# Pooled attention with a multiplicative FFN on one core: the FFN's products in 64-row tiles between the scores, attention in bursts of one head, a ring of exponentials twice as long

## The chip, the core and the metric

One Trainium2 chip, one of its cores, one launch. The metric is device time in microseconds (us): the median of the runs of the kernel. The engines are named as the profile names them: PE is TensorE (matmuls), PEld its weight loads, DVE is VectorE, ACT is ScalarE, POOL is GpSimd, SP is SyncE, which here only issues DMAs.

## The reference

Inputs are float32. q, k and v are [8 batches, 8 heads, 1152 positions, 64]. The FFN works on 4608 tokens (8 batches of 576), d_model 512, d_ff 1024.

```python
q_pool = q.reshape(B, H, S // 2, 2, D).mean(axis=3)          # 576 queries a head
scores = (1 / sqrt(D)) * q_pool @ k.T                        # 576 x 1152 a head
attn = softmax(scores, axis=-1)
x = (attn @ v).transpose(0, 2, 1, 3).reshape(B * 576, H * D) # 4608 x 512
h = ((x @ w1) * (x @ w2)) @ w3                               # 4608 x 1024
out = h @ w_out                                              # 4608 x 512
```

The kernel never forms h: it computes T = w3 @ w_out once (1024 x 512), and out = ((x @ w1) * (x @ w2)) @ T.

## The kernel before

**Pairs, steps and chunks.** Two heads of a batch make a pair P (32 pairs). The 1152 keys of a head are cut into 9 blocks of 128, and a pair has 9 steps (NJ), each of 576 queries (SQ) against one key block, for both heads. The steps of all pairs follow each other as one line of 32 x 9 x 576 columns, which is cut into 324 chunks of 512 columns (CH). A pair is 10.125 chunks long.

**Scores and exponentials.** `scores(c)` (line 229) makes one chunk: for each of the one or two steps that it touches, one matmul per head. A head has 64 features, so each is a matmul on 64 of the 128 rows of PE: head 0 on rows 0 to 63, head 1 on rows 64 to 127, into two PSUM banks of a tile `psc`, of which there are two (4 banks). `expo(c)` (line 235) is one ACT instruction over 128 x 1024 elements, from `psc` to a ring `er` in SBUF, which holds 9 chunks (RING 4608). PE can write a chunk's scores when ACT has read the chunk two before it.

**Attention times V.** `attend(J, i)` (line 248) takes 128 exponentials columns as weights and 65 columns of V (the 65th holds a constant, so that it sums the exponentials), on all 128 rows, for both heads. Its accumulator `po` has two banks, one per head. A pair has 9 x 5 x 2 = 90 of these matmuls, and there are 2880. After the last step of a pair `normalize(P)` takes the reciprocal (line 258) and multiplies (line 260) on DVE, and two DMA transposes (lines 265, 268) put the result into `xT`, the FFN's input.

**Keys and queries.** For the first nine pairs `prep_pe` (lines 203, 155) transposes queries and keys on PE through two PSUM banks, and DVE copies them out (lines 209 to 211). Later pairs go through DMA transposes (lines 131, 133). POOL issues the loads from HBM; `wosb` (w_out) and `w3h` (w3) are loaded early, `w1sb` and `w2sb` after them.

**The FFN.** It works in units of 512 tokens, nine in all (`gen_ffn`). A unit has 8 pairs of gate blocks: `pa` (line 347) is four matmuls on 128 rows with 512 columns, copied to SBUF by DVE (line 356); `pb` (line 360) is four, multiplied by that copy (line 365) into `gT`. Then come four row blocks `pp` (line 373) of eight matmuls each, scaled into SBUF (line 382) and stored by DMA (line 387). A unit thus has 96 matmuls. A unit can run when its tokens' pairs are done; seven units run beside the attention, and the last two and what is left of the seventh after it. All PSUM tiles of the FFN, of T (`gen_T`, line 313) and of the transposes of w3 (line 302) share two banks (tag `ff`).

**The order.** It is written out by hand, in the order of the code, for each engine. The loop goes over 162 iterations of two chunks: scores of both chunks, then the `attend` matmuls that are ready, then FFN matmuls as `fill` takes them from a list of generators, one matmul at a time, until a planned time `due` is reached, which grows by PACE0 or PACE1 (2.2, 2.19 us) an iteration. So a block of four FFN matmuls may be split over two iterations.

**PSUM** has 8 banks: 4 for `psc`, 2 for `ff`, 2 for `po`.

Of the kernel before, what the change touches and what calls it, by code (L numbers as in the profile page):

```python
# [10 lines left out]
ALU = mybir.AluOpType  # L11
# [7 lines left out]
RING = 4608  # L19
# [4 lines left out]
def kernel(  # L24
# [21 lines left out]
    T_MM, T_TR, T_SC, T_AV, T_PREP = 0.216, 0.06, 0.63, 0.061, 1.0  # L46
    PACE0, PACE1 = 2.2, 2.19
# [13 lines left out]
    w3T = const.tile([128, NF, NF, 128], FP16)  # L61
# [5 lines left out]
    seen = const.tile([1, 2], FP16)  # L67

# [6 lines left out]
    kst, vst, qst, kT, qT, qps = {}, {}, {}, {}, {}, {}  # L75

# [81 lines left out]
    def prep_first():  # L158
# [6 lines left out]
        ta = psum.tile([128, 1024], FP16, tag="ff", bufs=2, name="ta")  # L165
        tb = psum.tile([128, 1024], FP16, tag="ff", bufs=2, name="tb")
# [30 lines left out]
    def prep_pe(P):  # L197
        pp, o = P // 2, 64 * (P % 2)
        new_kq(P)
        t2 = psum.tile([128, 1024], FP16, tag="ff", bufs=2, name="t2")  # L200
        t1 = psum.tile([128, 1024], FP16, tag="ff", bufs=2, name="t1")
        for c in range(NJ):
            nc.tensor.transpose(t2[:, 128 + 64 * c:192 + 64 * c],  # L203
                                qps[pp][o:o + 64, c].rearrange("p u d -> p (u d)"),
                                ident[o:o + 64, o:o + 64])
        keys(P, t2, range(8, 9))
        keys(P, t1, range(0, 8))
        del kcs[P]
        nc.vector.tensor_copy(out=qT[P].rearrange("p c f -> p (c f)"), in_=t2[:, 128:704])
        nc.vector.tensor_copy(out=kT[P][:, 0:8].rearrange("p j f -> p (j f)"), in_=t1)  # L210
        nc.vector.tensor_copy(out=kT[P][:, 8], in_=t2[:, 0:128])
# [26 lines left out]
    po = {}  # L238

    def attend(J, i):  # L240

        P, j = divmod(J, NJ)
        if j == 0 and i == 0:
            po[P] = psum.tile([128, 2, 512], FP32, tag="po", bufs=1, name="po")
        f = 128 * i if i < 4 else SQ - 128
        r = (J * SQ) % RING + f
        for u in range(2):
            nc.tensor.matmul(  # L248
                po[P][:, u, VW * i:VW * i + D + 1],
                er[:, u, r:r + 128],  # L250
                vts[P % 4][:, u, j, 0:D + 1],
                start=(j == 0 and i == 0), stop=(j == NJ - 1 and i == 4),
                skip_group_check=True)

    def normalize(P):
        acc = po.pop(P)[:, :, 0:5 * VW].rearrange("p u (i w) -> p u i w", w=VW)
        rz = ab.tile([128, 2, 5, 1], FP32, tag="rz", bufs=2, name="rz")
        nc.vector.reciprocal(out=rz, in_=acc[:, :, :, D:D + 1])
        xn = ab.tile([128, 5, 2, D], FP16, tag="xn", bufs=3, name="xn")
        nc.vector.tensor_tensor(  # L260
            out=xn.rearrange("p i u d -> p u i d"), in0=acc[:, :, :, 0:D],
            in1=rz.to_broadcast([128, 2, 5, D]), op=ALU.mult)
# [7 lines left out]
            in_=xn[64:128, 4].rearrange("p u d -> p (u d)"))  # L270

# [22 lines left out]
    def bank(pre, wide):  # L294
        if not wide:
            return psum.tile([128, 512], FP32, tag="ff", bufs=2, name=pre)
        return psum.tile([128, 2, 512], FP32, tag="psc", bufs=2, name=pre)[:, 0, :]

    def w3_transpose(c):
        t = psum.tile([128, 1024], FP16, tag="ff", bufs=2, name="w3t")  # L300
        for a in range(NF):
            nc.tensor.transpose(t[:, 128 * a:128 * a + 128],  # L302
                                w3h[c // 4][:, c % 4, 128 * a:128 * a + 128], ident)
        nc.vector.tensor_copy(out=w3T[:, c].rearrange("p a f -> p (a f)"), in_=t)

    def gen_w3(c):
        w3_transpose(c)
        yield 8 * T_TR, 0

    def gen_T(c):  # L310
        pt = bank("pT", False)
        for a in range(NF):
            nc.tensor.matmul(pt, w3T[:, c, a, :], wosb[:, a, :],  # L313
                             start=(a == 0), stop=(a == NF - 1))
            if a < NF - 1:
                yield T_MM, NF - 1 - a
        nc.vector.tensor_copy(out=T16[:, c, :], in_=pt)
        yield T_MM, 0

    def last_rows(pp, gT, r0):  # L320
        osb = ffp.tile([128, dm], FP32, tag="osb", bufs=3, name="osb")
        for h in range(2):
            hs = slice(256 * h, 256 * h + 256)
            if h == 1:
                pp = bank("pp", False)
# [15 lines left out]
    def gen_ffn(t, tail):  # L341
        t0 = 512 * t
        gT = ffp.tile([128, NF, 512], FP16, tag="g", name="gT")
        for ft in range(NF):
            pa = bank("pa", tail and ft % 2)
            for mc in range(NC):
# [3 lines left out]
                if mc < NC - 1:  # L350
                    yield T_MM, NC - 1 - mc
            asb = ffp.tile([128, 512], FP32, tag="asb", name="asb")
            if tail:
                nc.scalar.copy(out=asb, in_=pa)  # L354
            else:
                nc.vector.tensor_copy(out=asb, in_=pa)  # L356
            yield T_MM, 0
            pb = bank("pb", tail and ft % 2)
            for mc in range(NC):
# [3 lines left out]
                if mc < NC - 1:  # L363
                    yield T_MM, NC - 1 - mc
            nc.vector.tensor_mul(out=gT[:, ft, :], in0=pb, in1=asb)  # L365
            yield T_MM, 0
        for i in range(4):
            pp = bank("pp", tail and i % 2)
            if tail and t == n_units - 1 and i == 3:
                last_rows(pp, gT, t0 + 384)  # L370
                return
            for ft in range(NF):
                nc.tensor.matmul(pp, gT[:, ft, 128 * i:128 * i + 128], T16[:, ft, :],  # L373
                                 start=(ft == 0), stop=(ft == NF - 1))
                if ft < NF - 1:
                    yield T_MM, NF - 1 - ft
            osb = ffp.tile([128, dm], FP32, tag="osb", bufs=3, name="osb")
            if tail:
                nc.scalar.activation(out=osb, in_=pp, func=AF.Copy, bias=0.0,
                                     scale=1.0 / (SCL * SCL))  # L380
            else:
                nc.vector.tensor_scalar_mul(out=osb, in0=pp, scalar1=1.0 / (SCL * SCL))  # L382

            for s in range(2):
                b, f = divmod(t0 + 128 * i + 64 * s, SQ)
                rows = out[b * SQ:(b + 1) * SQ, :].rearrange("(p c) m -> c p m", c=NJ)
                nc.sync.dma_start(out=rows[f // 64], in_=osb[64 * s:64 * s + 64, :])
            yield T_MM, 0
# [3 lines left out]
    NIT = NCHUNK // 2  # L392
# [19 lines left out]
    filler = []  # L412
    next_unit = 0
    busy = due = 0.0
    left = 0
    blocks = [(J, i) for J in range(NP * NJ) for i in range(5)]
    nb = 0

    def fill(until, settle=False):

        nonlocal busy, left
        while filler and (left if settle else busy < until):
            try:
                cost, left = next(filler[0])
                busy += cost
            except StopIteration:
                filler.pop(0)

    early = [(5, gen_w3, 0), (5, gen_w3, 1), (9, gen_T, 0), (9, gen_T, 1),
             (10, gen_w3, 2), (10, gen_w3, 3), (10, gen_T, 2), (11, gen_T, 3),  # L430
             (14, gen_w3, 4), (15, gen_w3, 5), (15, gen_T, 4), (15, gen_w3, 6),
             (15, gen_T, 5), (15, gen_w3, 7), (15, gen_T, 6), (15, gen_T, 7)]

    def pv(ready):
        for J, i in ready:
            attend(J, i)

    STAGE = {1: 0.39, 2: 1.35}
    PREP = {1: 0.55, 2: 1.5}
    closed = False  # L440
    for it in range(NIT):
        at = it * 2 * CH / PAIR
        while early and it >= early[0][0]:
            _, gen, c = early.pop(0)
            filler.append(gen(c))
        while next_unit < n_units:
            last_b = (512 * (next_unit + 1) - 1) // SQ
            if (last_b + 1) * 4 * PAIR + 3 * 2 * CH > it * 2 * CH:
                break
            filler.append(gen_ffn(next_unit, False))  # L450
            next_unit += 1
        ready = [b for b in blocks[nb:nb + 40]
                 if b[0] * SQ + min(128 * b[1] + 128, SQ) <= 2 * it * CH]
        last = [n for n, (J, i) in enumerate(ready) if J % NJ == NJ - 1 and i == 4]
        if last:
            ready = ready[:last[0] + 1]
        nb += len(ready)
        half = 0 if filler else len(ready) // 2
        scores(2 * it)
        expo(2 * it)  # L460
        if it == 0:
# [4 lines left out]
        pv(ready[:half])  # L466
        scores(2 * it + 1)
        expo(2 * it + 1)
        busy += T_SC
        due = (due if filler else busy - T_SC) + (PACE0 if it < 20 else PACE1)  # L470
        if it >= NIT - 6:
            due -= 0.25
# [20 lines left out]
        if todo or (last and left <= 2):  # L493
            fill(0, settle=True)
        elif closed:
            fill(min(due - T_AV * len(ready), busy + 3 * T_MM))
        closed = bool(last)
        pv(ready[half:])
        busy += T_AV * len(ready)
        if last:  # L500
            normalize(ready[-1][0] // NJ)
        if todo:
            prep_pe(prepped)
            busy += T_PREP
            prepped += 1
        else:
            fill(due)
    fill(0, settle=True)
    for J, i in blocks[nb:]:
        attend(J, i)  # L510
    normalize(NP - 1)
    for g in filler:
        for _ in g:
            pass
    while next_unit < n_units:
        for _ in gen_ffn(next_unit, True):
            pass
# [31 lines left out]
```

## Time and profile before

| what | value |
|---|---|
| median of 3 runs (lowest, highest) | 435.61 us (435.55, 436.33) |
| span of the profiled execution, first to last instruction | 433.2 us |
| granted TensorE clock over the span | 0.999 |
| PE busy | 418.4 us, 97% |
| ACT busy | 329.2 us, 76% |
| DVE busy | 208.6 us, 48% |
| POOL busy | 84.4 us, 19% |
| exponentials (ACT, line 235) | 324, from 8.3 us to the last start at 372.1 us |
| FFN matmuls, all lines | 856 of 512 columns and 16 of 256 |
| DVE reading one FFN bank of 512 columns | 690 ns |

The execution that was profiled has no time of its own apart from its span; the median lies 2.4 us above the span, and the working below takes these 2.4 us as fixed.

The page gives an engine's busy time as the union of its instructions. A matmul's duration there (379 ns for 512 columns) is from its first column in to its last result out, and the next one starts before that; what one costs in a row of them is the distance from start to start, which is read from the timeline. In the timeline equal instructions are merged: start, time from the first start to the last end, and the count.

### The profile page before, as it was taken

The page shows a single profiled execution, that of the slowest core. Times are in us where ns is not written, and L with a number is a line of the kernel's source. Part 1 is how long each engine was busy: PE and PEld are TensorE (multiplying, and loading weights), DVE is VectorE, ACT ScalarE, POOL GpSimd, SP SyncE. Part 2 cuts the span into 40 slices and gives each one's busy share as a digit, 9 for nine tenths or more (in the row PEclk, how much of TensorE's full clock was granted, in tenths as well). Part 3 has the DMA queues.
Part 4 walks back from the last instruction along what each step waited for, and adds up shares of the span by engine and source line. Part 5 has one row for each costly group of instructions (what it writes and reads, how often), then busy time and mean ns, then how long its engine had stood idle before and what let it go on. Part 6 is the DMA issues. An engine that isn't in the chain of part 4 may idle for free.

```text
span 433.2 us, 12222 instructions
## 1 busy us (share of the span) xinstructions
PE 418.4 (97%) x5194; PEld 226.5 (52%) x5194; DVE 208.6 (48%) x365; ACT 329.2 (76%) x351; POOL 84.4 (19%) x154
## 2 busy tenths in 40 slices
PE   4899999999999999999999999999999999999996
PEld 2556666555555555555555555555545555444443
DVE  2445555575455544545356545554465433544131
ACT  4998888878888888888888888888888888403332
POOL 8313333002222040122222222222222000000000
PEclk9999999999999999999999999999999999999999
DMA  8999999908999999999899899999979972030404
GB/s 122 205 196 199 190 190 204 176 15 115 144 176 134 143 139 201 152 143 124 164 176 135 133 159 182 142 144 136 196 129 138 147 120 39 17 80 17 98 1 97
DMA packets 94197, 58.67 MB, mean 135 GB/s; under 512 B 64832, under 2 KB 84544, under 8 KB 94144
## 3 DMA queue, kind: packets, MB, share of 16 engines
q0 software_dynamic: 26528, 33.56, 51.1%
q1 hardware_dynamic: 67456, 24.22, 34.7%
q8 instruction: 40, 0.66, 0.7%
q10 hardware_dynamic: 160, 0.13, 0.1%
q14 instruction: 13, 0.11, 0.1%
HBM read 67.11 MB, written 9.44 MB: 177 GB/s over the span
## 4 chain that ended last, share of the span: by engine, by line
PE 90%; ACT 4%; issue 2%; DMA 1%; DVE 1%; POOL 0%; SPq 0%; ACTq 0%; POOLq 0%
PE po L248 21%; PE psc L229 21%; PE pa L347 14%; PE pp L373 14%; PE pb L360 14%; ACT er L235 4%; PE pT L313 3%; PE t L155 1%; DMA kst<-in_k_dram 1%; PE w3t L302 1%; PE t L203 1%; DMA out_dram<-osb 1%; DVE xn L260 0%; PE tb L155 0%; POOL qst L82 0%
## 5 line engine op out<-in xcount | busy, mean ns | idle before, releaser
L235 ACT ACTIVATE er<-psc 128x1024 f16<-128x1024 f32 x324 | 313.0, 1021 | 52.8 <-PE psc L229 50.1
L248 PEld LDWEIGHTS <-er 128*128 128x128 f16 x2880 | 100.4, 97 | 36.8 <-issue 26.8
L248 PE MATMUL po<-vt,er 128*128 128x65 f16 x2880 | 116.4, 194 | 0.1
L229 PE MATMUL psc<-qT,kT 64*128 64x512 f16 (+7 forms) x1152 | 109.7, 288 | 4.6 <-ACT er L235 3.2
L229 PEld LDWEIGHTS <-kT 64*128 64x128 f16 x1152 | 43.9, 94 | 77.0 <-issue 65.5
L365 DVE TENSOR_TENSOR gT<-pb,asb 128x512 f16<-128x512 f32 x72 | 49.7, 690 | 69.4 <-PE pb L360 69.4
L360 PE MATMUL pb<-xT,w2sb 128*128 128x512 f16 x288 | 80.7, 379 | 0.1
L347 PE MATMUL pa<-xT,w1sb 128*128 128x512 f16 x288 | 79.4, 379 | 0.0
L373 PE MATMUL pp<-T,gT 128*128 128x512 f16 x280 | 69.3, 379 | 0.0
L356 DVE COPY asb<-pa 128x512 f32<-128x512 f32 x56 | 38.6, 690 | 42.7 <-PE pa L347 42.7
L382 DVE TENSOR_SCALAR osb<-pp 128x512 f32<-128x512 f32 x28 | 19.3, 690 | 47.2 <-PE pp L373 47.2
L347 PEld LDWEIGHTS <-w1sb 128*128 128x128 f16 x288 | 25.4, 97 | 25.6 <-issue 3.2
L138 POOL COPY seen<-kT 1x1 f16<-1x1 f16 x21 | 5.3, 250 | 170.0 <-DMA kT<-kc 170.0
L360 PEld LDWEIGHTS <-w2sb 128*128 128x128 f16 x288 | 25.0, 97 | 24.3 <-issue 3.9
L373 PEld LDWEIGHTS <-gT 128*128 128x128 f16 x280 | 24.3, 97 | 25.1 <-issue 2.5
L354 ACT COPY asb<-pa 128x512 f32<-128x512 f32 x16 | 9.4, 586 | 31.6 <-PE pa L347 31.6
L90 POOL DMA_DIRECT2D kst<-in_k_dram x33 | 23.6, 715 | 17.1 <-DVE xn L260 2.1
L260 DVE TENSOR_TENSOR xn<-po,rz 128x640 f16<-128x640 f32 x32 | 26.4, 824 | 1.1
L97 POOL DMA_DIRECT2D vst<-in_v_dram x32 | 23.2, 724 | 17.2 <-DVE kT L210 4.7
L114 DVE TENSOR_TENSOR qp<-qst 64x1152 f16<-64x1152 f16 x31 | 23.2, 749 | 3.4 <-DMA qst<-in_q_dram 2.9
L82 POOL DMA_DIRECT2D qst<-in_q_dram x32 | 20.4, 637 | 7.9 <-DMA w1sb<-in_moe_w_dram 2.8
L313 PE MATMUL pT<-wosb,w3T 128*128 128x512 f16 x64 | 16.6, 379 | 0.0
(44 smaller groups left out, 116.5 us busy)
## 6 DMA issues: line engine op xcount, KB each, us to landing
qst<-in_q_dram POOLq DMA_DIRECT2D x32, 288.0 KB, 6.7
vst<-in_v_dram POOLq DMA_DIRECT2D x32, 288.0 KB, 8.4
out_dram<-osb SPq DMA_DIRECT2D x70, 128.0 KB, 3.0
kst<-in_k_dram POOLq DMA_DIRECT2D x31, 288.0 KB, 5.3
w3h<-in_moe_w_dram POOLq DMA_DIRECT2D x4, 512.0 KB, 17.0
wosb<-in_moe_w_out_dram POOLq DMA_DIRECT2D x1, 1024.0 KB, 17.3
xT<-xn SPq DMA_TRANSPOSE x64, 4.2
w1sb<-in_moe_w_dram POOLq DMA_DIRECT2D x2, 512.0 KB, 17.0
```

The costliest lines, as they stand in the source:

```text
L90: nc.gpsimd.dma_start(out=kst[P][:, :, js[0]:js[1], :], in_=k[b, h0:h0 + 2].rearrange("u (p j) d -> p u j d", j=NJ)[:, :, js[0]:js[1], :])
L97: nc.gpsimd.dma_start(out=vst[P].rearrange("p u j d -> p u (j d)"), in_=v[b, h0:h0 + 2].rearrange("u (p j) d -> p u (j d)", j=NJ))
L229: nc.tensor.matmul(t[:, u, o:o + ln], kT[P][s, j, :], qv[s, f0:f0 + ln], start=True, stop=True)
L235: nc.scalar.activation(out=er[:, :, r:r + CH], in_=psc.pop(c), func=AF.Exp, bias=0.0, scale=SCALE)
L248: nc.tensor.matmul(po[P][:, u, VW * i:VW * i + D + 1], er[:, u, r:r + 128], vts[P % 4][:, u, j, 0:D + 1], start=(j == 0 and i == 0), stop= ...
L260: nc.vector.tensor_tensor(out=xn.rearrange("p i u d -> p u i d"), in0=acc[:, :, :, 0:D], in1=rz.to_broadcast([128, 2, 5, D]), op=ALU.mult)
L313: nc.tensor.matmul(pt, w3T[:, c, a, :], wosb[:, a, :], start=(a == 0), stop=(a == NF - 1))
L347: nc.tensor.matmul(pa, w1sb[:, mc, ft * 128:ft * 128 + 128], xT[:, mc, t0:t0 + 512], start=(mc == 0), stop=(mc == NC - 1))
L356: nc.vector.tensor_copy(out=asb, in_=pa)
L360: nc.tensor.matmul(pb, w2sb[:, mc, ft * 128:ft * 128 + 128], xT[:, mc, t0:t0 + 512], start=(mc == 0), stop=(mc == NC - 1))
L365: nc.vector.tensor_mul(out=gT[:, ft, :], in0=pb, in1=asb)
L373: nc.tensor.matmul(pp, gT[:, ft, 128 * i:128 * i + 128], T16[:, ft, :], start=(ft == 0), stop=(ft == NF - 1))
```

## The change

- **FFN in half-height tiles.** Each FFN matmul on 128 rows becomes two on 64 rows (h = 0 and h = 1) into the same PSUM bank. `Block` holds the bank of one block. `group()` issues the four products of a block part: for each, the half h = 0, and beside it the half h = 1 of the product six places earlier (`lag`). The two then lie on different rows and in different banks. When the four halves h = 0 of a part are issued, DVE copies one element of the bank (`handed`, line 348 after), so that the first half h = 1 waits for them. There is at most one group, or half a block of T (`T_half`), per chunk, and not one matmul at a time. The planned time grows by PACE = 1.06 us a chunk.
- **Attention in bursts.** `attend(P, u)` issues all 45 matmuls of one head of a pair at once, the first head one chunk after the pair's last chunk, the second five chunks after it. The accumulator has one bank instead of two; reciprocal and multiplication run per head.
- **Ring doubled.** RING is 9216, 18 chunks.
- **PSUM banks.** The FFN, T and the transposes of w3 take turns on three banks (`spare`) instead of two; `prep_pe` is split into `prep_pe_q` and `prep_pe_k`, one chunk apart, and its tiles now share the one bank of `po`.
- **Order.** In each chunk: scores, exponentials, then one of: a burst, a part of the preparation, one transpose of w3; then a `T_half` or a group. T's first parts and the transposes of w3 stand at other chunks (`early`), units of the FFN start about five chunks later, and the last row block of a unit is held back into the next unit. What is left after the last chunk runs in whole 128-row matmuls (`tail_ffn` is the former tail of `gen_ffn`).

```diff
-RING = 4608
+RING = 9216
...
-    T_MM, T_TR, T_SC, T_AV, T_PREP = 0.216, 0.06, 0.63, 0.061, 1.0
-    PACE0, PACE1 = 2.2, 2.19
+    T_GRP, T_SC, T_PV, T_PREP, T_W3, PACE = 0.866, 0.219, 1.56, 0.7, 0.67, 1.06
...
+    spare = [0, 1, 2]
+
+    def bank(pre, dt=FP32, n=None):
+        if n is None:
+            n = spare.pop(0)
+            spare.append(n)
+        return psum.tile([128, 2048 // (4 if dt == FP32 else 2)], dt, tag=f"ff{n}", bufs=1,
+                         name=pre)
...
-        t2 = psum.tile([128, 1024], FP16, tag="ff", bufs=2, name="t2")
+        t2 = psum.tile([128, 1024], FP16, tag="po", bufs=1, name="t2")
...
+    def prep_pe_k(P):
+        t1 = psum.tile([128, 1024], FP16, tag="po", bufs=1, name="t1")
...
-    def attend(J, i):
...
+    def attend(P, u):
+        po = psum.tile([128, 512], FP32, tag="po", bufs=1, name="po")
+        for j in range(NJ):
+            r0 = ((P * NJ + j) * SQ) % RING
+            for i in range(5):
...
+        nc.vector.reciprocal(out=rz, in_=acc[:, :, D:D + 1])
...
+        nc.vector.tensor_tensor(
+            out=xn[:, :, u, :], in0=acc[:, :, 0:D],
+            in1=rz.to_broadcast([128, 5, D]), op=ALU.mult)
+        if u == 0:
+            return
...
+    class Block:
...
+        def product(self, part, n, h, lhsT, rhs):
+            if self.n is None:
+                self.n = spare.pop(0)
+                self.t = bank(self.pre, n=self.n)
+            s = slice(0, 128) if h is None else slice(64 * h, 64 * h + 64)
+            last = h != 0 and part == self.n_parts - 1 and n == 3
+            nc.tensor.matmul(self.t, lhsT(s), rhs(s), start=(h != 1 and part == 0 and n == 0),
+                             stop=last, skip_group_check=True)
+            if last:
+                self.then(self.t)
+                spare.append(self.n)
+            elif n == 3:
+                nc.vector.tensor_copy(out=handed, in_=self.t[0:1, 0:1])
...
+    def group():
+        for x in parts.pop(0):
+            product(x, 0)
+            lag.append(x)
+            if len(lag) > 6:
+                product(lag.pop(0), 1)
...
+    early = [(10, 0), (11, 1), (19, 2), (20, 3), (28, 4), (30, 5), (32, 6), (34, 7)]
+    bursts = sorted([(last_chunk(P) + (1 if u == 0 else 5), P, u)
+                     for P in range(NP) for u in range(2)])
...
+        due = (due if parts or halves else busy) + PACE
         busy += T_SC
...
+        if bursts and c >= bursts[0][0]:
+            attend(*bursts.pop(0)[1:])
+            busy += T_PV
+        elif half_prepped is not None:
+            prep_pe_k(half_prepped)
...
+        elif todo:
+            prep_pe_q(prepped)
...
+        elif early and c >= early[0][0] and len(w3T) < 4:
+            w = early.pop(0)[1]
+            w3_transpose(w)
+            busy += T_W3
+            halves.extend([(w, 0), (w, 4)])
+        if halves and busy + 0.5 * T_GRP <= due:
+            T_half(*halves.pop(0))
+            busy += T_GRP
+        elif parts and not (early or halves) and busy + 0.5 * T_GRP <= due:
+            group()
+            busy += T_GRP
```

`then` is DVE's reading of the bank: the copy of `pa` (line 357 after), the multiplication with `pb` (362) or the scaling of `pp` (370). The products of all three are line 342 after, T is 320, the scores 239, the bursts 257, the transposes of queries 210 and of keys 163.

## The prediction

> **What bounds the kernel now.** I read the chain that ended last first, then the busy time by stage, then the timeline of one iteration, and last the timeline of the stretch where PE runs FFN blocks alone. The chain and two groups of the page:
>
> ```profile
> PE 90%; ACT 4%; issue 2%; DMA 1%; DVE 1%; POOL 0%; SPq 0%; ACTq 0%; POOLq 0%
> ...
> L235 ACT ACTIVATE er<-psc 128x1024 f16<-128x1024 f32 x324 | 313.0, 1021 | 52.8 <-PE psc L229 50.1
> ...
> L365 DVE TENSOR_TENSOR gT<-pb,asb 128x512 f16<-128x512 f32 x72 | 49.7, 690 | 69.4 <-PE pb L360 69.4
> ```
>
> PE is the chain. ACT waits for scores (50.1 us); alone it would need 0.92 us a chunk (in the timeline four exponentials take 3.78 us and one 1.02, so they start (3.78 - 1.02) / 3 apart), 298 us for 324, where the loop takes 364 us. DVE mostly waits for products to end. The stage 130 to 250 us, from the answer by windows (length, then busy time of PE, PEld, DVE, ACT, POOL):
>
> ```profile
> 130.00:250.00 120.00, 119.63 (x1571) 63.75 (x1569) 61.03 (x104) 102.75 (x107) 25.03 (x50) 1.00 1.04 150
> ```
>
> PE is never free there, so whatever is added to or taken from PE's order moves the end one for one. What PE pays between its work shows in the timeline of one iteration (start, duration, count):
>
> ```profile
> 199.71 0.39 PE L229 MATMUL psc<-qT,kT 64*128 64x512 f16 x2
> 200.03 0.72 PE L248 MATMUL po<-vt,er 128*128 128x65 f16 x18
> 200.59 0.59 PE L360 MATMUL pb<-xT,w2sb 128*128 128x512 f16 x2
> 201.02 0.81 PE L373 MATMUL pp<-T,gT 128*128 128x512 f16 x3
> 201.76 0.61 PE L229 MATMUL psc<-qT,kT 64*128 64x64 f16 x8
> ```
>
> A product of 512 columns lasts 0.38, and three take 0.81, so they start (0.81 - 0.38) / 2 = 0.216 apart. The third starts at 201.45, but the score after it only at 201.76: 0.31 instead of 0.216. Going from 128 rows to 64 costs 0.095. The other way, scores of 512 columns start at 199.71 and the first 128-row matmul at 200.03: 0.32, so 0.10 too much. I take 0.098 per change of height. Two scores on different rows take 0.39 together, no more than one: they run side by side.
>
> The next four lines are from the stretch after the exponentials, where blocks alternate on two banks:
>
> ```profile
> 376.07 1.02 PE L360 MATMUL pb<-xT,w2sb 128*128 128x512 f16 x4
> ...
> 376.93 1.03 PE L347 MATMUL pa<-xT,w1sb 128*128 128x512 f16 x4
> 377.13 0.69 DVE L365 TENSOR_TENSOR gT<-pb,asb 128x512 f16<-128x512 f32 x1 [0.42 <-PE pb L360]
> ...
> 377.87 1.02 PE L360 MATMUL pb<-xT,w2sb 128*128 128x512 f16 x4
> ```
>
> This is the price of a bank's return. The block's last product starts at 376.07 + 1.02 - 0.38 = 376.71; DVE starts 0.04 after its end, reads for 0.69, and PE refills the bank 0.05 after that, at 377.87. From the last product's start to the next block in that bank: 1.16 us. The `pa` block between would have let PE go on at 376.93 + 4 x 0.216 = 377.79, so PE waited 0.08.
>
> **The change part by part.** I counted PE's instructions in the order of both kernels.
>
> *Changes of height.* Neighbours on PE differ in rows 353 times before and 207 after (62 into and 62 out of the bursts, the rest at T, the transposes of w3 and the preparation). 146 x 0.098 = 14.3 us are saved, all of it after the FFN begins; ahead of it there are 85 before and 94 after.
>
> *Products in halves.* 640 of the 856 products run as two halves. A pair costs 0.216 as before if the next pair follows as closely. For scores, 64 + 448 + 128 columns take 0.61 - 0.33 = 0.28 from the first start to the last in the line at 201.76, against 0.27 at the products' rate: some 4 ns a pair. The bounds are 1 and 11 ns, and 4 gives 640 x 0.004 = +2.6. At the start six halves have no partner yet: 6 x 0.216 = +1.3. Weight loads double in number, on PEld, busy 52%; those of scores hide behind the matmuls today.
>
> *A bank's return.* With three banks in turn, a block needs the bank of the third block before it. That block's last half runs beside the second product of the block directly before. So PE has, until it wants the bank, three pairs (0.66), and, when the next group comes in the next chunk, one chunk's scores (0.23): 0.89 against 1.16, a wait of 0.27. In the order after, 103 of 159 groups follow a group in the very next chunk. Behind the waiting product stand, in PE's order, the next scores, so ACT's work comes later too, and PE has no slack to regain it. Where a burst or an empty chunk lies between, 1.16 is covered. Bounds per case: 0.15, if part falls together with waits of scores for ACT, and 0.28. I take 0.24, near the direct reading: 103 x 0.24 = +24.7.
>
> *One bank for attention and preparation.* A burst's bank is free 0.19 (its last matmul) + 0.04 + 0.24 (reciprocal, line 258) + 0.49 (multiplication, 320 columns scaled from 824 ns for 640 and 690 for 512) + 0.05 = 1.01 after the last matmul's start. `prep_pe_q` follows in the next chunk, after 0.03 + 0.10 + 0.23: a wait of 0.65, in 7 of 8 cases, 4.6. `prep_pe_k` waits for the copies of lines 209 and 211 (0.46 + 0.21, overlapping by 0.08): 0.22 + 0.04 + 0.59 + 0.05 = 0.90, less 0.46 for two changes of height and a chunk, 0.44, eight times, 3.5. Sum +8.1; bounds 5 and 10.
>
> *T earlier than its weights.* T's first product stands behind the scores of chunk 14; before, it came at 27.50. Chunk 14's scores run at about 21.9 in this profile. `wosb` was issued at 9.40 and took this long:
>
> ```profile
> wosb<-in_moe_w_out_dram POOLq DMA_DIRECT2D x1, 1024.0 KB, 17.3
> ```
>
> POOL's order up to there is unchanged, so it lands at 26.7 and PE stands with scores and bursts queued behind: 26.7 - 21.8 = +4.9 (bounds 3 and 6).
>
> *At no cost.* The 188 `handed` copies take about 0.2 each on DVE (the nearest row, line 211, has 215 ns): 38 us on an engine with 208.6 busy. The waiting half comes 0.22 + 0.23 + 2 x 0.22 = 0.89 after the last h = 0 half, and the copy is back after 0.38 + 0.04 + 0.2 + 0.05 = 0.67. Behind a pair's three preparation copies on DVE (0.74 + 0.45 + 0.45) that cover is gone; I put up to 6 us of it into the high end. The doubled ring costs nothing, since ACT never waited for it visibly. Reciprocals and multiplications per head add 64 - 32 short instructions to DVE. On SP the 64 transposes into `xT` wait for the second head; units of the FFN begin eleven chunks after their pairs, over 10 us, against 4.2 us to landing. The 2880 attention matmuls stay at 29 to 30 ns. The tail only trades places: what is left out of the loop or put into it costs the same products.
>
> Sum: -14.3 + 2.6 + 1.3 + 24.7 + 8.1 + 4.9 = +27.3. Span 433.2 + 27.3 = 460.5; with the 2.4 us by which the median exceeds the span, 463.
>
> Two rules bear on this. The Trainium skill's "TensorEngine Tiling (Array Packing)", section Restrictions and Gotchas, warns that row tiling raises PSUM pressure and that different row tiles may not use one PSUM bank at a time; it names no price, and speaks against this change in the place where I find the cost. The skill's "TensorE: Matmul & The Clock Gate", section Back-to-back issue gap, gives about 131 ns per product of 512 columns in streams with weight loads; by that the wait would be 1.16 - 3 x 0.131 - 0.23 = 0.54 and its sum 55 us, but the trace has 0.216 throughout, and the trace decides.
>
> **The rivals.** *Banks come back in time* (about 439): the 24.7 falls away because DVE's answer is covered, for instance if waits of scores for ACT take its place. 463 - 24.7 = 438.6. Against it stands the 0.08 wait at 377.87, with more cover (0.86 from four products, plus nothing to read before it) than I find missing here.
>
> *Faster: the round trips over DVE all vanish* (about 430). If PE had some other 0.3 to 0.7 us between releasing a bank and wanting it, neither the FFN's banks nor the attention's bank would stop it: 463 - 24.7 - 8.1 = 430, the 14.3 of saved changes prevailing. It decides where both waits together are below 14.3 - 2.6 - 1.3 - 4.9 = 5.5 us, say under 0.05 per following group and nothing at the shared bank. For it speaks that bursts of 1.3 us keep PE away from the FFN's banks; against it, that 103 groups have no burst ahead.
>
> *The halves do not run side by side* (about 600): 640 x 0.216 = +138. The two scores in 0.39 speak against it.
>
> **How the numbers follow.** A measurement of this kernel can tell about 0.2%, 0.9 us. My sum: 0.82, with all terms at their low bounds -15 + 0.7 + 1.3 + 15.5 + 5 + 3 = +10.5 (446), and at their high ones -13.5 + 7 + 1.3 + 28.8 + 10 + 6 = +39.6 (475, and 476 with a little of DVE's 6 us). Banks in time 0.07; faster 0.06; between these two and within 0.2%, 0.02; not side by side 0.03. So faster 0.06, same 0.02, slower 0.07 + 0.82 + 0.03 = 0.92. The range 446 to 476 holds 0.82.
>
> **What would show it.** Right: changes of height only around bursts, T and preparation; waits of line 342 for DVE of about 0.27, together near 25 us; `t2` and `t1` (lines 210, 163) waiting for DVE, 8 us; `pT` (line 320) waiting some 5 us for `wosb`; the last exponential near 400 us instead of 372; some 1.19 us a chunk between 130 and 250 us instead of 1.12. Wrong: PE without waits on DVE at line 342, halves starting 0.2 apart, or line 342 waiting for `handed` in the middle of a group.

## The result, and the profile after

The changed kernel takes 462.39 us (median of 4 runs, 460.9 to 463.99); the kernel before, run beside it, 435.97 us (435.55 to 437.72). The ratio is 1.0586, with a 95% interval of 1.0532 to 1.064: slower, 0.6 us from the predicted 463.0. The profiled execution took 460.9 us, its span 459.1, against the 460.5 of the sum. Each comparison below has its own runs of the kernel before on its chip, so ratios are what compares across them.

The page of the profile after: span, busy time of each engine, the chain by engine, and four groups (line, engine, operation, count | busy, mean ns | idle time before them and what ended it).

```profile
span 459.1 us, 13873 instructions
...
PE 421.1 (92%) x5834; PEld 247.1 (54%) x5834; DVE 235.9 (51%) x617; ACT 330.4 (72%) x351; POOL 81.1 (18%) x154
...
PE 74%; ACT 10%; DVE 7%; DMA 4%; issue 2%; POOL 2%; ACTq 0%; SPq 0%; DVEq 0%; POOLq 0%
...
L245 ACT ACTIVATE er<-psc 128x1024 f16<-128x1024 f32 x324 | 314.2, 1027 | 79.6 <-PE psc L239 78.5
...
L342 PE MATMUL pb<-xT,w2sb 64*128 64x512 f16 x448 | 97.9, 376 | 5.6 <-DVE handed L348 3.0
L342 PE MATMUL pa<-xT,w1sb 64*128 64x512 f16 x448 | 97.9, 376 | 2.8 <-DVE handed L348 0.2
...
L342 PE MATMUL pp<-T,gT 64*128 64x512 f16 (+1 forms) x416 | 73.7, 376 | 2.7 <-DVE handed L348 1.1
```

PE had 90% of the chain and now has 74%: 10% went to ACT, 7% to DVE, 4% to a DMA. PE has things to wait for, and ACT's idle time ahead of scores has grown from 50.1 to 78.5 us. The page's idle time for line 342 adds up to 11.1 us only, because an engine counts as busy until its last matmul's results are out, 0.16 after the next one could have started. To see the whole wait one has to go from start to start. For this I took every PE instruction of the trace, gave it the distance that its predecessor needs (0.216 for 512 columns, 0.096 more at a change of height), and counted what it starts later than that (by over 25 ns) as a wait. This is my own sum over the trace:

| PE's waits, us | before | after |
|---|---|---|
| FFN products (line 342 after) | below 1 | 21.1 (75 times, median 0.29) |
| scores for ACT (line 239 after) | 13.4 (median 0.147) | 18.6 (74 times, median 0.255) |
| preparation `t2`, `t1` (lines 210, 163) | below 1 | 8.3 |
| `pT` for `wosb` (line 320) | 0 | 2.6 |
| all | 15.5 | 53.2 |

The waits grow by 37.7. Some 2.4 of that is not waiting: near the start PE ran at half rate for longer (until 21.8 us instead of 12.5, last section), and the wider spacing there counts as waits in this sum (2.1 us before, 4.5 after). Changes of height fall by 146; in this trace one costs 0.093 into and 0.096 out of a 128-row matmul, so 13.7 are saved. 37.7 - 13.7 = 24.0, and the spans differ by 459.1 - 433.2 = 25.9; the first six halves without a partner are 1.3 of the rest.

One wait of line 342, from the timeline after (start, duration, count; weight loads left out):

```profile
204.09 0.80 PE L342 MATMUL pb<-xT,w2sb 64*128 64x512 f16 x5
...
204.53 0.38 PE L342 MATMUL pa<-xT,w1sb 64*128 64x512 f16 x1
...
204.73 0.38 PE L342 MATMUL pb<-xT,w2sb 64*128 64x512 f16 x1
204.73 0.69 DVE L362 TENSOR_TENSOR gT<-pb,asb 128x512 f16<-128x512 f32 x1 [0.65 <-PE pb L342]
...
204.75 0.38 PE L342 MATMUL pa<-xT,w1sb 64*128 64x512 f16 x1
204.95 0.40 PE L239 MATMUL psc<-qT,kT 64*128 64x448 f16 x4
...
205.34 0.14 DVE L348 COPY handed<-pb 1x1 f32<-1x1 f32 x1
205.47 0.80 PE L342 MATMUL pa<-xT,w1sb 64*128 64x512 f16 x5
```

The first two products of the group at 204.09 run beside the last two halves of the `pb` before it, the other two beside halves of `pa`. DVE then reads the older `pb` from 204.73 to 205.42, and its bank is the next in turn. The scores behind the group start at 204.95 and would have let the next group start at 205.18; it starts at 205.47, 0.05 after the read. No bracket marks this 0.29. The `handed` copy beside it ends after the product has started, so it isn't what was waited for, though the page names it: of the 75 waits, 73 end within 0.14 after a DVE read of a bank, and 2 at a `handed`. The stage 130 to 250 us, as for the profile before (length, then busy time of PE, PEld, DVE, ACT, POOL with counts, granted clock):

```profile
130.00:250.00 120.00, 114.32 (x1743) 68.99 (x1739) 68.38 (x192) 96.86 (x101) 23.94 (x50) 1.00 0.93 150
```

101 exponentials in 120 us are 1.19 a chunk, where there were 107 (1.12). The last exponential starts at 400.2 us, 372.1 before.

### The profile page after: what moved, and what is told of

It is laid out like the page before. It is cut to its first block, busy times and chain, and to the rows that moved or that the text cites. A ratio compares the mean times of both kernels' runs of the same rounds, so it can differ in the third digit from the quotient of the medians.

```text
span 459.1 us, 13873 instructions
## 1 busy us (share of the span) xinstructions
PE 421.1 (92%) x5834; PEld 247.1 (54%) x5834; DVE 235.9 (51%) x617; ACT 330.4 (72%) x351; POOL 81.1 (18%) x154
## 4 chain that ended last, share of the span: by engine, by line
PE 74%; ACT 10%; DVE 7%; DMA 4%; issue 2%; POOL 2%; ACTq 0%; SPq 0%; DVEq 0%; POOLq 0%
PE po L257 20%; PE psc L239 15%; ACT er L245 10%; PE pb L342 9%; PE pp L342 8%; PE pa L342 7%; DMA wosb<-in_moe_w_out_dram 4%; PE pT L320 3%; PE pb L440 3%; PE pa L433 3%; PE pp L450 2%; DVE handed L348 2%; PE t L163 1%; DVE xn L269 1%; DVE qp L122 1%
## 5 line engine op out<-in xcount | busy, mean ns | idle before, releaser
L245 ACT ACTIVATE er<-psc 128x1024 f16<-128x1024 f32 x324 | 314.2, 1027 | 79.6 <-PE psc L239 78.5
L239 PE MATMUL psc<-qT,kT 64*128 64x512 f16 (+7 forms) x1152 | 120.9, 290 | 7.5 <-ACT er L245 2.7
L342 PE MATMUL pb<-xT,w2sb 64*128 64x512 f16 x448 | 97.9, 376 | 5.6 <-DVE handed L348 3.0
L342 PE MATMUL pa<-xT,w1sb 64*128 64x512 f16 x448 | 97.9, 376 | 2.8 <-DVE handed L348 0.2
L257 PE MATMUL po<-vt,er 128*128 128x65 f16 x2880 | 99.4, 194 | 0.8 <-DVE xn L269 0.8
L342 PE MATMUL pp<-T,gT 64*128 64x512 f16 (+1 forms) x416 | 73.7, 376 | 2.7 <-DVE handed L348 1.1
L357 DVE COPY asb<-pa 128x512 f32<-128x512 f32 x56 | 38.7, 691 | 24.1 <-PE pa L342 23.7
L342 PEld LDWEIGHTS <-w2sb 64*128 64x128 f16 x448 | 33.7, 94 | 28.7 <-issue 12.1
L342 PEld LDWEIGHTS <-w1sb 64*128 64x128 f16 x448 | 33.7, 94 | 22.3 <-issue 6.0
L265 DVE RECIPROCAL rz<-po 128x5 f32<-128x5 f32 x64 | 12.4, 194 | 61.2 <-PE po L257 61.2
L342 PEld LDWEIGHTS <-gT 64*128 64x128 f16 (+1 forms) x416 | 27.0, 94 | 23.1 <-issue 6.2
L269 DVE TENSOR_TENSOR xn<-po,rz 128x320 f16<-128x320 f32 x64 | 31.5, 491 | 2.4 <-DVE rz L265 0.3
L98 POOL DMA_DIRECT2D kst<-in_k_dram x33 | 23.7, 718 | 28.5 <-DVE kc L158 14.4
L443 DVE TENSOR_TENSOR gT<-pb,asb 128x512 f16<-128x512 f32 x16 | 11.1, 692 | 23.5 <-PE pb L440 23.5
## 6 DMA issues: line engine op xcount, KB each, us to landing
w3h<-in_moe_w_dram POOLq DMA_DIRECT2D x4, 512.0 KB, 15.5
```

Of the source, the lines that this page charges most:

```text
L98: nc.gpsimd.dma_start(out=kst[P][:, :, js[0]:js[1], :], in_=k[b, h0:h0 + 2].rearrange("u (p j) d -> p u j d", j=NJ)[:, :, js[0]:js[1], :])
L239: nc.tensor.matmul(t[:, u, o:o + ln], kT[P][s, j, :], qv[s, f0:f0 + ln], start=True, stop=True)
L245: nc.scalar.activation(out=er[:, :, r:r + CH], in_=psc.pop(c), func=AF.Exp, bias=0.0, scale=SCALE)
L257: nc.tensor.matmul(po[:, VW * i:VW * i + D + 1], er[:, u, r:r + 128], vts[P % 4][:, u, j, 0:D + 1], start=(j == 0 and i == 0), stop=(j == ...
L269: nc.vector.tensor_tensor(out=xn[:, :, u, :], in0=acc[:, :, 0:D], in1=rz.to_broadcast([128, 5, D]), op=ALU.mult)
L342: nc.tensor.matmul(self.t, lhsT(s), rhs(s), start=(h != 1 and part == 0 and n == 0), stop=last, skip_group_check=True)
```

## The experiments

Each is an edit of the kernel after.

**1. A shorter lag.** With a lag of four halves, the last half of a block lies further from the group that wants its bank; with seven it lies nearer. The diff is that of four; the runs with seven and five have 7 and 5 in that place.

```diff
-            if len(lag) > 6:
+            if len(lag) > 4:
```

> The changed kernel with the half h = 1 issued four products after h = 0 instead of six; nothing else differs. Theory (a bank's return over DVE stops PE): a block's last half now runs beside the fourth product of the next block, so the bank has five pairs' and two chunks' time to come back, more than the 1.16 us it needs, and the 21 us of waits before first products go; the first half h = 1 now stands 0.45 us after the last h = 0, where the copy `handed` (0.13 us in the changed kernel's profile) is back after 0.60, so some 0.15 us come at each of about 100 groups that follow a group directly. Expected 445 to 450 us against 462.4. Rival (the wait for `handed`, the handing over between the halves, is what costs): the handing over gets less time, so slower than 462.4, some 470 to 480. Second rival (the bursts of 45 matmuls starve ScalarE and PE waits for exponentials): no difference, 460 to 464.

> The changed kernel with the half h = 1 issued seven products after h = 0 instead of six; nothing else differs. Theory (bank's return): the last half runs one product later, the next user of the bank has two pairs and one chunk of scores, 0.67 us, against 1.16, so the wait per following group grows from 0.27 to about 0.49; 100 groups give 17 to 22 us more: 479 to 485 us. Rival (handing over): it has more time, so faster than 462.4, some 450 to 458. Second rival (bursts starve ScalarE): no difference, 460 to 464.

> The changed kernel with the half h = 1 five products after h = 0. Theory: the bank has four pairs and a chunk of scores, 1.09 us against 1.16, so 0.07 at each of about 100 following groups in place of 0.27; the hand-over has 0.66 against 0.60 and is covered. Expected 445 to 452 us, near the kernel with four. Rival (only a lag of four, where at most two blocks are open, frees the banks; with five three blocks are still open): the gain is half or less, 455 to 462.

| lag | time, us | ratio (95%) | waits of line 342, us | median wait |
|---|---|---|---|---|
| 4 | 450.59 | 1.0288 (1.0222 to 1.0355) | 6.8 | 0.22 (17 waits) |
| 5 | 452.30 | 1.0362 (1.0305 to 1.0419) | 13.3 | 0.077 |
| 6 (after) | 462.39 | 1.0586 (1.0532 to 1.064) | 21.1 | 0.29 |
| 7 | 480.52 | 1.0986 (1.0924 to 1.1048) | 40.0 | 0.506 |

From five to seven the median wait goes 0.08, 0.29, 0.51: one pair of 0.216 a step, as it must if the wait is what is left of DVE's answer after PE's cover. The same place with a lag of seven:

```profile
201.74 0.40 PE L239 MATMUL psc<-qT,kT 64*128 64x448 f16 x4
201.74 0.69 DVE L357 COPY asb<-pa 128x512 f32<-128x512 f32 x1 [0.86 <-PE pa L342]
...
202.48 1.02 PE L342 MATMUL pb<-xT,w2sb 64*128 64x512 f16 x7 [0.35 <-DVE handed L348]
```

DVE starts its read with the scores, not 0.22 ahead of them as in the profile after, and the product comes at 202.48 instead of 201.97. The rivals fall: if the handover copies were the cost, a shorter lag would have made it slower, and if the bursts were, it would have changed nothing. At lags of four and five the time is 0.6 and 0.3 above the ranges. With five, the waits of line 342 hold seven of over 0.6 us, together 8.4, which are of the kind with other work ahead on DVE, shown further down. With four, PE ran at half rate for twice 3.4 us in the profile (last section), so the 1.7 us between four and five tell little. The 0.15 that was expected there at each hand-over is not paid: in 240 of the 636 pairs the second half starts 0.15 to 0.21 after the first, and the pairs still follow each other every 0.216.

**2. The same banks and bursts, whole products.** The group issues each product on 128 rows, as before the change.

```diff
-            product(x, 0)
-            lag.append(x)
-            if len(lag) > 6:
-                product(lag.pop(0), 1)
+            product(x, None)
```

> The changed kernel with each group as four matmuls on 128 rows in place of the halves: no halves, no `handed`, no lag; bursts, banks, order of chunks and pace as in the changed kernel. Theory: a block ends in its own group, so no bank's return is waited for (-21 us), no pair spacing and unpaired halves (-4); two changes of row height come with each of 159 groups, 318 x 0.098 = +31, part of which falls where PE waits for exponentials anyway (PE's waits for ScalarE are 18.6 us in the changed kernel). Expected 456 to 468 us; no waits of FFN products for DVE in the profile. Rival (bursts and the shared attention bank cost all of it, the halves are as good as meant): the halves' gain is lost and nothing is won, 462 + 31 = 490 or more.

It took 464.19 us, ratio 1.0611 (1.0542 to 1.0681). Changes of height are 525 instead of 207, and the waits of line 342 shrink to 0.4 us:

```profile
130.00:250.00 120.00, 120.00 (x1498) 59.66 (x1497) 64.80 (x131) 98.00 (x101) 21.90 (x46) 1.00 0.95 149
```

PE is busy throughout, and still there are 101 exponentials, as in the profile after. So halves have their worth: against the lag of four, 318 more changes x 0.094 = +29.9, waits -15.1, no unpaired halves -0.9 (four at that lag), together +13.9, where the two kernels differ by 464.19 - 450.59 = 13.6. At a lag of six the 29.9 that halves save in changes are spent on waits: 20.7 for banks, and 8.9 of scores for ACT (18.6 against 9.7 here, with a median of 0.06: the changes of height fill time in which PE would otherwise wait).

**3. T behind its weights.** No part of T before chunk 19.

```diff
-        if halves and busy + 0.5 * T_GRP <= due:
+        if halves and c >= 19 and busy + 0.5 * T_GRP <= due:
```

> The changed kernel with T's first products held until chunk 19, as late as in the kernel before; nothing else differs. Theory: the 2.6 us (2.5 in the profile's idle time) that PE stands waiting for `wosb`, and the wait for exponentials that the stop causes after it, go; expected 457 to 460 us, no wait of line 320 for `wosb`. Rival (early work is limited by loads and ScalarE anyway): the wait comes back elsewhere, 461 to 463.

460.87 us, ratio 1.054 (1.0473 to 1.0606): 0.9 above the range, and the interval overlaps that of the kernel after, so it doesn't tell. The timeline shows part of why. First the kernel after, then this one (PE only):

```profile
20.28 2.21 PE L257 MATMUL po<-vt,er 128*128 128x65 f16 x45
...
26.21 1.02 PE L320 MATMUL pT<-wosb,w3T 128*128 128x512 f16 x4 [2.52 <-DMA wosb<-in_moe_w_out_dram]
...
28.79 1.54 PE L257 MATMUL po<-vt,er 128*128 128x65 f16 x45
```

```profile
20.50 2.65 PE L257 MATMUL po<-vt,er 128*128 128x65 f16 x45
23.08 0.61 PE L239 MATMUL psc<-qT,kT 64*128 64x192 f16 x4
...
26.14 1.54 PE L257 MATMUL po<-vt,er 128*128 128x65 f16 x45
```

The wait for `wosb` is gone. But the first burst takes 2.65 or 2.21 us where a burst takes 1.54: PE starts its matmuls at half the rate there, in this kernel until 23.9 us. Moreover chunks 18 to 60, where the held products now stand, took 51.8 us instead of 50.6, and the profile has a stretch at half rate from 351.6 to 355.0 us and 23.9 us of waits at line 342. So I took the wait away in another way:

```diff
     load_w3(0)
-    load(2)
     load_w(wosb, moe_w_out)
+    load(2)
```

> The changed kernel with the load of `wosb` issued ahead of the third pair's loads on GpSimd's queue; nothing else differs. Theory: `wosb` lands about 2 us earlier, and T's first product waits 0 to 1 us for it instead of 2.6: 459.5 to 461 us. Rival (the third pair's loads come later and its preparation waits): 462 to 465.

459.83 us, ratio 1.0528 (1.0494 to 1.0562), within what was expected. The interval still overlaps with that of the kernel after, but the stage tells: `pT` starts straight after the scores, and chunks 12 to 18 take 8.0 us instead of 10.6 (6.0 before), 2.6 less, which is the wait and also the difference of the medians.

**4. Preparation on the FFN's banks.** The tiles `t2` and `t1` no longer share the attention's bank; the FFN hardly uses its own so early.

```diff
-        t2 = psum.tile([128, 1024], FP16, tag="po", bufs=1, name="t2")
+        t2 = bank("t2", FP16)
...
-        t1 = psum.tile([128, 1024], FP16, tag="po", bufs=1, name="t1")
+        t1 = bank("t1", FP16)
```

> The changed kernel, with the transposes of keys and queries (t2, t1) written into the FFN's three banks in turn instead of the attention's one bank; nothing else differs. Theory: the waits of these transposes for VectorE (4.7 us at line 210 and about 3 at line 163 in the changed kernel, by the starts in its trace) go, since no FFN runs yet: 454 to 458 us against 462.4. Rival (these early chunks are limited by ScalarE or loads): no difference, 460 to 464.

460.74 us, ratio 1.0544 (1.0504 to 1.0583): a miss, above the range. Part of it may be that PE ran at half rate from 25.4 to 32.2 us in this profile (last section). The waits themselves had gone. In the profile after, the queries' transposes stand behind the multiplication that empties the bank; in this one they follow the scores at once:

```profile
30.26 0.39 PE L239 MATMUL psc<-qT,kT 64*128 64x448 f16 x4
31.14 0.43 PE L210 MATMUL t<-ident,qp 64*128 64x64 f16 x9 [0.49 <-DVE xn L269]
```

```profile
32.86 0.39 PE L239 MATMUL psc<-qT,kT 64*128 64x448 f16 x4
33.09 0.42 PE L210 MATMUL t<-ident,qp 64*128 64x64 f16 x9
```

Waits at lines 210 and 163 fall from 8.3 to 1.4 us, but those of scores for ACT rise by 1.9 and those of line 342 by 1.4. Both kernels were run again side by side, the one after unchanged (e9) and this one (e10), to settle whether these waits are worth their length or less:

> The changed kernel as it is, on the same chip as the next one, to compare with. Expected 460 to 464 us.

> The transposes of keys and queries on the FFN's banks, as before, now beside the changed kernel on one chip. Theory (the waits at lines 210 and 163 add to PE's chain in full): 7 to 8 us below the changed kernel. Rival (they stand where PE would otherwise wait for an exponential or a load, so only part of them is paid): 1.5 to 4 us below it. The chunks 18 to 60, where all but one of these transposes stand, took 50.9 us in the changed kernel's profile and 47.9 with the other banks, which speaks for the rival with about 3.

464.25 us (ratio 1.0648, 1.06 to 1.0696) and 459.54 us (1.0523, 1.0476 to 1.0569): 4.7 apart, between the two expectations. PE's waits agree with it: 7.1 less at lines 210 and 163, but 0.8 more of scores for ACT, 1.0 more at line 342, and in all 54.8 against 49.6, 5.2 less. So a part of these waits only stands in the place of others. The stages put the gain lower still. Chunks 18 to 60 took 50.6 us in both profiles of the kernel after and 48.05 in both with the other banks, 2.6 less. Chunks 12 to 18 took 9.7 us in e10 against 10.6 in the first profile of the kernel after, 0.9 less; in e9 they took 11.6, because PE ran at half rate there for 3.4 us. Without that, 3.5 of the 7.1 us were gained, which is within the rival's range.

**5. All together.** Lag four, preparation on the FFN's banks, `wosb` ahead of `load(2)`, and T's accumulator keeps its bank until it is copied out (it has to, now that others take turns between its halves).

```diff
-            pts[c] = bank("pT")
+            n = spare.pop(0)
+            pts[c] = bank("pT", n=n)
+            ptn[c] = n
...
+            spare.append(ptn.pop(c))
```

> The changed kernel with a lag of four, the transposes of keys and queries and T's accumulators on the FFN's banks (a T accumulator keeps its bank out of the turn until it is copied), and the load of `wosb` issued ahead of the third pair's loads. Theory: the terms add: 450.6 (lag of four alone) less 5 to 8 for the preparation and 2 to 4 for T's wait: 438 to 444 us, no faster than the kernel before, because scores still wait some 19 us for exponentials (13 before) and the hand-over some 5. Rival (the terms overlap, PE waits elsewhere instead): 446 to 451. Rival (the saved changes of row height show in full once the waits are gone): below 430.

440.60 us (12 runs, 437.48 to 443.21), ratio 1.0079 (1.0045 to 1.0114): 21.8 of the 26.4 us are undone (one by one the edits gave 11.8 + 4.7 + 2.6 = 19.1), but it doesn't beat the kernel before. PE's waits are 30.8 us: 15.3 more than before, 6.8 of them of scores for ACT (20.2) and 7.2 of FFN products, of which five long ones, between 180 and 352 us, make 5.0. 15.3 - 13.7 + 0.9 (four halves without a partner) = 2.5, of a difference in span of 438.9 - 433.2 = 5.7; the other 3.2 stay open. PE's half rate near the start, until 21.9 us here (last section), is a candidate of which these waits hold only a part; it was not tested by itself.

## Why the prediction was right, step by step

It had the mechanism and the size. Some of its terms were off, and that their errors nearly cancelled is luck.

- **Changes of height: right.** Predicted -14.3, measured 146 x 0.094 = -13.7, and experiment 2 confirms the price.
- **Halves side by side: right, the spacing mis-sized.** Predicted +4 ns a pair, 2.6 in all; the median distance from pair to pair is 215 ns, so 0. The "64 + 448 + 128 columns" that gave 4 ns were three short matmuls, each with its own start. In the profile after, the partners of a pair start 2 to 20 ns apart, all but one (204.516 and 204.533, for example; the timeline merges equal rows and shows only the second by itself). "Halves starting 0.2 apart", named as a mark of being wrong, would not have been one: with a lag of four many do (experiment 1), and the rate is two in each 0.216 there too.
- **A bank's return: right mechanism, price and count mis-sized in opposite ways.** Where PE waits in full, it is 0.29 (read directly 0.27, taken as 0.24), but it does so in 57 places, not 103. In the trace 103 groups come with one chunk's scores between them and the group before, as counted ahead. 57 of these waited, by some 0.29 or more. 40 waited 0.05 at most because the scores just ahead of them had waited for ACT, which gave DVE its time; the low bound of 0.15 was meant for that. Six did not wait. Four waits of 1.1 to 1.3 us (4.5 of the 21.1) are of another kind, and the prediction had them, for `handed` copies, as "up to 6 us" behind preparation copies. Here it is the bank read that comes late (timeline after):

```profile
215.12 0.38 PE L342 MATMUL pb<-xT,w2sb 64*128 64x512 f16 x1
215.13 0.74 DVE L122 TENSOR_TENSOR qp<-qst 64x1152 f16<-64x1152 f16 x1
...
215.80 0.45 DVE L131 COPY vt<-vst 128x1152 f16<-128x1152 f16 x1
...
216.17 0.68 DVE L357 COPY asb<-pa 128x512 f32<-128x512 f32 x1
...
216.90 0.80 PE L342 MATMUL pb<-xT,w2sb 64*128 64x512 f16 x5 [0.91 <-DVE handed L348]
```

  PE's product at 216.90 waits for the read that ends at 216.85, and that stood behind two copies for the next pair. Measured in all 21.1 against 24.7; a lag of four got 11.8 us of the time back.
- **The shared bank: the waits right, their worth not.** 8.1 predicted, 8.3 measured, but 4.7 gained when they were removed, 3.5 by stage. The step that failed is that the sum took each wait at its full length: experiment 4 shows scores and products waiting more where the bank waits less.
- **T for `wosb`: half.** 4.9 predicted, 2.5 in the trace and 2.6 when removed. `wosb` landed at 26.2 (predicted 26.7); it was PE that came late, at 23.7 instead of 21.9, and its work up to there had run at half rate for longer (until 21.8 us instead of 12.5).
- **What the sum lacked: scores waiting for ACT, +5.2.** Half of it comes after 30 us (from 10.3 to 12.9) and goes with the bursts: these waits come, in the median, 3.04 us after a burst's first matmul. A burst keeps PE away from scores for 1.5 us, ACT runs dry, then does four chunks in a row, and PE stands until the first of them is read, at 199.27 (timeline after):

```profile
196.29 1.54 PE L257 MATMUL po<-vt,er 128*128 128x65 f16 x45
...
197.76 0.61 PE L239 MATMUL psc<-qT,kT 64*128 64x512 f16 x6
...
198.25 3.77 ACT L245 ACTIVATE er<-psc 128x1024 f16<-128x1024 f32 x4 [0.78 <-PE psc L239]
...
199.33 0.40 PE L239 MATMUL psc<-qT,kT 64*128 64x128 f16 x4
```

  The last line would have come at 199.07, after the products of 198.85. "Attention in bursts" was costed only by its changes of height. The scores' median wait rises from 0.147 to 0.255. In experiment 2, with the same bursts, it is 0.06, so what a burst costs depends on what else PE has to do until ACT is back. Splitting the bursts would test this by itself; it wasn't tried. The other half, 2.6, stands in the first 22 us, in the profile after all ahead of the first burst (20.28), and 1.2 of it is the half rate of the next point.
- **PE's half rate near the start: not in the sum.** By my sum over the trace it costs 6.2 us in the profile after and 3.3 before. 2.4 of these 3 us are inside the waits counted above.
- **The cancelling.** Against the sum, in waits: bank -3.6, spacing -2.6, shared bank +0.2, `wosb` -2.3, changes +0.6, together -7.7; scores for ACT +5.2. 27.3 - 7.7 + 5.2 = 24.8, where the spans differ by 25.9. These errors of opposite sign are why the time came so close; the 0.6 us does not say that the terms were that exact.
- **Handed copies: at no cost, right.** They last 134 ns (0.2 was estimated), and 2 of 75 waits end at one.
- **The rivals.** "Halves not side by side" and "banks back in time" are refuted by the 216 ns and the 21.1 us. The faster one needed both waits below 5.5 us. Experiment 5 comes near that with 7.2 at the FFN's products and 0.5 at the preparation, and yet ends at 440.6, not at 430: the scores' waits for ACT, which no case had as a term, take 6.8 us more than before, 4.2 of them after 30 us.

## What to carry to other kernels

When products are split into halves that finish at different times, count from the last half, not from the last product issued: what matters is how many pairs PE still has between a bank's last write and its next first one, against the consumer's whole round trip (0.38 result, 0.04, 0.69 read, 0.05 here), and here one pair more or less of lag moved the time by up to 18 us. Before adding up waits on an engine that is the chain, look for the next resource behind it (here ACT, through two `psc` tiles): part of each wait only takes the place of another, so waits removed gave half to all of their length. And anything done in a burst needs its own term, for the engine that it starves meanwhile.

## What the runs showed of the hardware

PE at half rate was not expected. In the profile before, the matmuls at the start are spaced doubly until 12.5 us; in the profile after, throughout until 21.8 us (the first burst above, 2.21 instead of 1.54), although the granted clock in the rows of that stage reads 1.00: the trace's record of the clock begins only at 12.5 and 21.8 us. It returned in the middle of a run: with a lag of four, DVE stood in its queue behind a copy that waited 2.73 us for its load, the `handed` copy stood behind that, and PE idled for 1.90 us. From 261.17 on seven halves take 1.82 instead of 1.02, and here the row has the clock, 0.57 (the timeline, PE and DVE, and then one row by windows, as above):

```profile
258.90 0.46 DVE L131 COPY vt<-vst 128x1152 f16<-128x1152 f16 x1 [2.73 <-DMA vst<-in_v_dram]
...
260.09 1.02 PE L342 MATMUL pp<-T,gT 64*128 64x512 f16 x7 [1.90 <-DVE handed L348]
...
261.17 1.82 PE L342 MATMUL pp<-T,gT 64*128 64x512 f16 x7
```

```profile
261.00:265.00 4.00, 4.00 (x29) 2.14 (x24) 0.69 (x5) 2.05 (x2) 0.00 (x0) 0.57 1.34 166
```

So a wait of 1.9 us was followed by about 3.4 us (261.17 to 264.53) at half rate, which loses some 1.7 us more. It does not always come. In the profiles of the kernel after and of the ten runs above, PE idles for over 1.2 us eleven times between 15 and 400 us. Half rate follows seven of these times, of 1.89 to 2.49 us, six times for 3.4 us and once for 6.8; it does not follow the other four, of 1.72, 1.85, 2.52 and 2.71 us. Each of the seven stretches begins during such an idle time or at most 1.3 us after it. The wait for `wosb` in the kernel after shows both cases: it took 2.16 us in the profile of e9 and 2.52 in the first one. The rows by windows behind it, e9 first, have a granted clock of 0.50 and of 1.00:

```profile
25.80:29.20 3.40, 3.04 (x10) 0.82 (x10) 0.00 (x0) 0.59 (x1) 1.00 (x2) 0.50 1.15 209
```

```profile
26.20:30.00 3.80, 3.79 (x56) 2.04 (x56) 0.69 (x1) 2.05 (x2) 1.43 (x2) 1.00 1.15 209
```

Two executions of one kernel can thus differ by 1.7 us, so differences of that size are better read by stage, beside the granted clock. The Trainium skill's "TensorE: Matmul & The Clock Gate", Part 1, describes a clock gate that halves the rate after an idle window of about 3.4 us and lifts it after a busy one; the 3.4 us of slow work agree, but here idle times of 1.9 to 2.5 us were enough seven times, and four others of 1.7 to 2.7 us were not.
